# Gated linear attention and MLP: first loads in other pieces, and the fifth unit in another PSUM bank

## Chip, cores and metric

The kernel runs on one core of a Trainium2 chip. The metric is the device time of one execution in microseconds. It is written in Bass with every instruction's place on its engine given by a hand-written list; semaphores are derived from the dependencies. The engines are TensorE (PE), VectorE (DVE), ScalarE (ACT), GpSimd (POOL) and SyncE (SP, which only issues DMAs). Each runs its own list in order and waits for semaphores of the others.

## The reference

2048 tokens `x` of width 512. Branch `a` is linear attention with 32 heads of 16, whose features are the softmax of a projection and of its negative; branch `b` is a ReLU MLP with 1376 hidden columns. A sigmoid gate per token mixes them. (Types are bfloat16; heads and transposes are left out here.)

```python
def reference(x, wqkv, w_phi, wo, w1, w2, gate_w):
    g = sigmoid((x * gate_w).sum(-1, keepdims=True))
    q, k, v = split_heads(x @ wqkv)
    pq, pk = (einsum("bhsd,hdf->bhsf", t, w_phi) for t in (q, k))
    phi_q = concatenate([softmax(pq), softmax(-pq)], -1)
    phi_k = concatenate([softmax(pk), softmax(-pk)], -1)
    kv = einsum("bhsf,bhsd->bhfd", phi_k, v)
    z = einsum("bhsf->bhf", phi_k)
    o = einsum("bhqf,bhfd->bhqd", phi_q, kv) / (einsum("bhqf,bhf->bhq", phi_q, z)[..., None] + 1e-6)
    a = merge_heads(o) @ wo
    b = maximum(x @ w1, 0) @ w2
    return g * a + (1 - g) * b
```

## The kernel before

**Tiles.** Tokens are handled in 4 chunks of 512 and 16 tiles of 128. `XT` holds x transposed (512 columns as 4 slices of 128 partitions). Chunks 1 to 3 are transposed by DMA. Chunk 0 is loaded as it is, into a slot of the later feature buffer `FT` (seen as `XN`), and PE turns it in 128x128 blocks (`xt{m}{n}`: tile m, half n); ACT and DVE copy the blocks to `XT` (`xe{m}{n}`).

**Units.** A list of 48 units goes through PSUM. Unit `h{c}_{k}` (line 397) is the hidden block k of chunk c, 4 matmuls of 512 columns; `rl{c}_{k}` on ACT is its ReLU into `HT`. The eleventh block, k = 10, has 96 hidden rows and one more, the gate's logit, which DVE copies out (`gr{c}`, line 464); it goes through DRAM (`g1`, `g2`) to come back by token. Four units `f0_{j}` in chunk 2 fold `w_phi` into the query weights (line 374); the same for the keys (`f1_{j}`) is done near the start, outside the list of units. The units' order is chunk 0 with 10 blocks; chunk 1 with 10 and then both eleventh blocks, `h0_10` and `h1_10`; chunk 2 with 11 and the 4 folds; chunk 3 with 11. So `h3_10` is unit 47, counted from 0.

**Banks.** Of eight PSUM banks, the units use 3, 4, 5 (`HB`) and, for unit 3, bank 2; `freed[b]` remembers what has to be done before bank b is used anew:

```python
GB4 = (*HB, 2)
b = GB4[n] if n < 4 else HB[(n - 4) % len(HB)]
...
freed[b] = (f"rl{a}_{k}",)
if k == KT - 1:
    ...
    freed[b] += (f"gr{a}",)
```

Banks 0, 1, 6, 7 (`XB`, `FB`) serve the turning of chunk 0 and the key folds, later 0 and 1 the projections and 6 and 7 the key-value sums. After the units, the output tiles `b{m}` (second MLP matmul, 11 matmuls, line 628) and `a{m}` (attention output, line 634) take banks `AB = (3, 4, 5, 2)` in turn, and b0 to b2 wait for what `freed` names last for their bank:

```python
war = [f"oe{m - len(AB)}"] if m >= len(AB) else [f"ve{NT - 1}"] if ab == 2 else list(freed[ab])
```

**The opening.** The first chunk's hidden blocks 0 to 3 begin before it is all there: `hh00`, `hh01`, `hh1`, `hh2`, `hh3` (line 403) are the slices j of the contraction for tiles 0 and 1, each wanting its slice of W1's first 512 columns; `hr0`, `hr1` and the units `h0_0` to `h0_3` (line 409) are the rest. Six warming matmuls (`warm0`, line 258) run before data is there.

**The queues.** Loads are issued by SP and ACT. An issue takes its place in the engine's list. Behind the first ones SP issues `w1b` (W1's next 512 columns), `wphi`, `wkT` (key weights, transposed by DMA, wanted by the key folds), `w1c`, `wv` and the transposed chunks.

**The middle.** Work on keys (`pr_k`, `ev`, `mx`, `mn`, `t1`, `t2`, `ex`, `sm`, `rc`, `nm`) ends in `kv0` to `kv15` (PE, line 563). DVE then masks the sums (`kn0`, `kn1`, line 594; `kz0`, `kz1`, line 596). Queries go the same way, are transposed by DMA (`tq`), and `nd{m}_{h}` (PE, line 606) makes numerators and denominators, `rd` and `o` (DVE, lines 613 and 615) divide, `to` transposes, `a{m}` follows, `oe{m}` (ACT) scales and `st{m}` stores. In the lists this part reads as follows, with what comes before and after left out:

```python
"pe":  "... v15 kv14 h3_10 pr_q5 kv15 b0 nd0_0 nd0_1 b3 nd1_0 nd1_1 b2 pr_q6 a0 nd2_0 nd2_1 b1 nd3_1 ..."
"dve": "... sm_q1 kn1 kn0 kz0 kz1 rc_q1 mn_q4 gr3 rd0_1 rd0_0 o0_0 o0_1 sm_q2 rd1_0 ..."
```

## Time and profile before

| | |
|---|---|
| median of 3 runs | 151.53 us (151.14 to 152.31) |
| span of the profiled execution, first to last instruction | 150.2 us |
| PE busy | 145.2 us, 97% |
| DVE, POOL, ACT busy | 76%, 73%, 61% |
| granted TensorE clock | 0.9 or more in all 40 slices |
| loads: HBM read | 4.42 MB |

The time of the profiled execution itself is not listed beside its span; the median of the runs is 1.3 us above the span, for what lies around it. In a line of the timeline the columns are the start, the busy time (of a group, from its first start to its last end), engine, source line, operation, output and input, shape, count, and in brackets the idle time just before and what ended it. PEld is PE's loading of weights, which overlaps its matmuls; SPq and ACTq are DMA issues. The DMA view gives the time from issue to landing by size and queue.

### The profile page before, as it was taken

The numbers are of one execution on the slowest core, as the hardware profiler recorded it, in microseconds if no ns is written. First come the engines' busy times: TensorE is split into PE (matmuls) and PEld (weight loads), VectorE is DVE, ScalarE is ACT, GpSimd is POOL, SyncE is SP. The second block draws the span as 40 slices with busy tenths as digits, with TensorE's granted clock in tenths as the row PEclk, the third lists the DMA queues.
The fourth block names the chain that finished last, engine by engine and source line by source line (L and its number), as shares of the span: only waits on it lengthen the run. The fifth ranks groups of instructions, "written<-read, shape, count | busy, mean of one in ns | idle before, by whom it ended". The sixth has DMA issues, their size and how long they took to land.

```text
span 150.2 us, 2515 instructions
## 1 busy us (share of the span) xinstructions
PE 145.2 (97%) x944; PEld 74.2 (49%) x961; DVE 113.4 (76%) x168; ACT 92.2 (61%) x127; POOL 109.4 (73%) x71
## 2 busy tenths in 40 slices
PE   7899999999999999999999999999999999999992
PEld 3664444445554465445444545445444454454461
DVE  2433666999899949979999899999999969436301
ACT  3356769799969766698983937446546551310151
POOL 3000499999999999999999999998999791330000
PEclk9999999999999999999999999999999999999999
DMA  4999995000005602300000230476698774986251
GB/s 146 280 179 233 213 203 108 0 0 0 7 1 132 218 4 66 103 0 0 4 0 0 56 86 18 92 175 140 174 110 173 179 209 105 109 212 140 64 162 53
DMA packets 46307, 15.59 MB, mean 104 GB/s; under 512 B 39796, under 2 KB 46292, under 8 KB 46296
## 3 DMA queue, kind: packets, MB, share of 16 engines
q1 hardware_dynamic: 43560, 12.99, 42.0%
q10 hardware_dynamic: 2736, 2.45, 5.1%
q8 instruction: 7, 0.11, 0.4%
q14 instruction: 4, 0.03, 0.1%
HBM read 4.42 MB, written 2.11 MB: 43 GB/s over the span
## 4 chain that ended last, share of the span: by engine, by line
PE 93%; DMA 3%; issue 1%; ACT 1%; SPq 1%; DVE 0%
PE PS L628 24%; PE PS L397 23%; PE PS L502 18%; PE PS L482 9%; PE PS L634 9%; PE PS L563 3%; PE PS L606 3%; DMA W<-in_B_w_dram 3%; PE PS L649 2%; PE PS L374 1%; ACT HT L460 1%; PE PS L403 1%; PE PS L660 1%; SPq L272 1%; PE PS L409 0%
## 5 line engine op out<-in xcount | busy, mean ns | idle before, releaser
L542 POOL TENSOR_TENSOR TS<-PB,MX 128x1024 bf16<-128x1024 bf16 (+1 forms) x18 | 30.9, 1723 | 14.9 <-DVE MX L533 14.9
L397 PE MATMUL PS<-XT,W 128*128 128x512 bf16 (+1 forms) x156 | 38.3, 379 | 0.2
L628 PE MATMUL PS<-W,HT 128*128 128x512 bf16 (+1 forms) x160 | 37.5, 379 | 0.3
L549 DVE TENSOR_REDUCE ZB<-FT 128x128 f32<-128x2048 bf16 (+1 forms) x18 | 36.6, 2031 | 1.0 <-ACT FT L547 1.0
L547 ACT ACTIVATE FT<-TS 128x2048 bf16<-128x2048 bf16 (+1 forms) x18 | 30.9, 1718 | 7.7 <-POOL TS L542 7.5
L542 POOL TENSOR_TENSOR TS<-MN,PB 128x1024 bf16<-128x1024 bf16 (+1 forms) x18 | 30.9, 1724 | 0.8 <-DVE MN L535 0.8
L502 PE MATMUL PS<-WP,XT 128*128 128x512 bf16 x124 | 30.0, 379 | 0.2
L556 POOL TENSOR_TENSOR FT<-FT,SC 128x2048 bf16<-128x2048 bf16 (+1 forms) x9 | 29.5, 3290 | 0.0
L460 ACT ACTIVATE HT<-PS 128x512 bf16<-128x512 f32 (+1 forms) x44 | 24.7, 597 | 5.8 <-PE PS L397 4.9
L628 PEld LDWEIGHTS PS<-W,HT 128*128 128x128 bf16 (+1 forms) x165 | 15.5, 98 | 17.1
L533 DVE TENSOR_REDUCE MX<-PB 128x64 bf16<-128x1024 bf16 (+1 forms) x18 | 19.5, 1085 | 5.8 <-ACT PB L529 5.7
L397 PEld LDWEIGHTS PS<-XT,W 128*128 128x128 bf16 (+1 forms) x160 | 15.6, 101 | 16.5
L679 ACT ACTIVATE OSB<-PS,OMG 128x512 bf16<-128x512 f32 x15 | 10.2, 687 | 20.3 <-PE PS L634 20.3
L535 DVE TENSOR_REDUCE MN<-PB 128x64 bf16<-128x1024 bf16 (+1 forms) x18 | 19.3, 1084 | 2.3 <-ACT PB L529 2.3
L529 ACT ACTIVATE PB<-PS 128x1024 bf16<-128x1024 f32 (+1 forms) x18 | 16.7, 927 | 6.7 <-PE PS L502 3.8
L502 PEld LDWEIGHTS PS<-WP,XT 128*128 128x128 bf16 x128 | 12.1, 98 | 13.9 <-DVE WP L344 0.4
L579 POOL TENSOR_TENSOR FT<-FT,SR 128x1024 bf16<-128x1024 bf16 (+1 forms) x9 | 15.6, 1739 | 0.7
L482 PE MATMUL PS<-WV,XT 128*128 128x512 bf16 x62 | 16.0, 379 | 0.1
L634 PE MATMUL PS<-WO,OT 128*128 128x512 bf16 x58 | 14.2, 378 | 0.1
L615 DVE SCALAR_TENSOR_TENSOR OTM<-PS,EG,RD 128x256 bf16<-128x256 f32 x32 | 13.8, 463 | 0.2
L613 DVE RECIPROCAL RD<-PS 128x16 f32<-128x16 f32 x32 | 6.5, 235 | 9.0 <-PE PS L606 8.8
L491 ACT ACTIVATE VS<-PS 128x512 bf16<-128x512 f32 x16 | 9.6, 603 | 4.8 <-PE PS L482 4.7
(50 smaller groups left out, 97.8 us busy)
## 6 DMA issues: line engine op xcount, KB each, us to landing
out_dram<-OSB ACTq DMA_DIRECT2D x15, 128.0 KB, 2.1
W<-in_B_w_dram SPq DMA_DIRECT2D x1, 1280.0 KB, 6.7
W<-in_B_w_dram SPq DMA_DIRECT2D x1, 512.0 KB, 5.6
WV<-in_A_wqkv_dram SPq DMA_DIRECT2D x1, 512.0 KB, 4.7
WO<-in_A_wo_dram SPq DMA_DIRECT2D x1, 512.0 KB, 4.7
FT<-in_A_x_dram SPq DMA_DIRECT2D x3, 128.0 KB, 4.0
W<-in_B_w_dram SPq DMA_DIRECT2D x1, 352.0 KB, 3.9
W<-in_B_w_dram ACTq DMA_DIRECT2D x2, 128.0 KB, 3.7
```

Source lines behind the costliest of these rows:

```text
L397: last = q.matmul(PS[0:m, b, :], W1[:, j, k * P:k * P + m], XT[:, j, chunk(c)], start=(j == 0), stop=(j == ND - 1))
L460: add(f"rl{a}_{k}", "act", lambda q, a=a, k=k, b=b, rows=rows: q.activation(HT[0:rows, k, chunk(a)], PS[0:rows, b, :], ACT.Relu), (prev,), ...
L482: last = q.matmul(PS[:, 2, :], XT[:, j, m * P:(m + 1) * P], WV[:, j, :], start=(j == 0), stop=(j == ND - 1))
L502: last = q.matmul(PS[:, n, :], XT[:, j, m * P:(m + 1) * P], WP[:, s, j, :], start=(j == 0), stop=(j == ND - 1))
L533: add(f"mx_{J}", "dve", lambda q, sl=sl, w=w, i=pbg: q.tensor_reduce(MX[:, sl, 0:w * H], i, AX.X, ALU.max), (f"ev_{J}", old("t1")), dur=0. ...
L535: add(f"mn_{J}", "dve", lambda q, sl=sl, w=w, i=pbg: q.tensor_reduce(MN[:, sl, 0:w * H], i, AX.X, ALU.min), (f"ev_{J}", old("t2")), dur=0. ...
L542: add(f"{tn}_{J}", "pool", lambda q, o3=o3, a3=a3, b3=b3: q.tensor_tensor(o3, a3, b3, ALU.subtract), (f"{'mx' if sg == 0 else 'mn'}_{J}", ...
L547: add(f"ex_{J}", "act", lambda q, fs=fs, ts=ts, w=w: q.activation(FT[:, fs, 0:w * F], TS[:, ts, 0:w * F], ACT.Exp), (f"t1_{J}", f"t2_{J}", ...
L549: add(f"sm_{J}", "dve", lambda q, fs=fs, sl=sl, w=w: q.tensor_reduce(ZB[:, sl, 0:2 * w * H], FT[:, fs, 0:w * F].rearrange("p (g d) -> p g ...
L556: add(f"nm_{J}", "pool", lambda q, f3=f3, sl=sl, w=w: q.tensor_tensor(f3, f3, SC[:, sl, 0:2 * w * H].unsqueeze(2).to_broadcast([P, 2 * w * ...
L628: last = q.matmul(PS[:, ab, :], HT[0:r, k, m * P:(m + 1) * P], W2[0:r, k, :], start=(k == 0), stop=False)
L634: last = q.matmul(PS[:, ab, :], OT[:, m % NOT, t, :], WO[:, t, :], start=False, stop=(t == ND - 1))
```

## The change

Five edits go together.

- Chunk 0 is loaded in two pieces, both on SP, in each of which partition p takes rows 2p and 2p + 1 of 256 rows, so a packet is 2 KB and no longer 1 KB. Tile m of chunk 0 thus holds every second row, and the stores of tiles 0 to 3 go to the same rows (`stored`).
- W1's first 512 columns come in three pieces on ACT: slice 0, slice 1, and slices 2 and 3 in one. Before, x and these slices were spread over SP (x00, w1a0, w1a2, x02, x03) and ACT (x01, w1a1, w1a3).
- SP's later loads follow right behind the two pieces of x, so they go out earlier.
- On PE, `hh2` stands behind `xt31` and no longer ahead of `xt20`.
- Unit 4 (`h0_4`) takes bank 6 in place of bank 3, and the units behind it take `HB` counted from 5. `f1_2`, which uses bank 6 too, waits for `rl0_4`, and `rl0_4` moves ahead of `fe1_1` on ACT. The definition of the key folds moves behind that of the units.

```diff
 "sp":
-        "x00 w1a0 w1a2 x02 x03 w1b wphi wkT w1c wv x1 x2 wqT x3 gw ...
+        "x0a x0b w1b wphi wkT w1c wv x1 x2 wqT x3 gw ...
 "act":
-        "x01 w1a1 w1a3 xe00 xe10 xe20 xe30 rl0_0 rl0_1 rl0_3 rl0_2 fe1_1 fe1_3 rl0_5 rl0_4 ev_k0 ...
+        "w1a0 w1a1 w1a2 xe00 xe10 xe20 xe30 rl0_0 rl0_1 rl0_3 rl0_2 rl0_4 fe1_1 fe1_3 rl0_5 ev_k0 ...
 "pe":
-        "warm0 xt00 xt01 xt10 xt11 hh00 hh01 hh1 hh2 xt20 xt21 xt30 xt31 hh3 hr0 hr1 ...
+        "warm0 xt00 xt01 xt10 xt11 hh00 hh01 hh1 xt20 xt21 xt30 xt31 hh2 hh3 hr0 hr1 ...

+        def stored(m):
+            if m < 4:
+                return o2[m // 2 * 2 * P:(m // 2 + 1) * 2 * P, :].rearrange("(p n) d -> p n d", n=2)[:, m % 2, :]
+            return o2[m * P:(m + 1) * P, :]

-        load_x(0, "sp", 2.95)
-        load_x(1, "act", 3.1)
-        load_w(0, "sp", 3.2)
-        load_w(1, "act", 3.4)
-        load_w(2, "sp", 3.8)
-        load_w(3, "act", 3.95)
-        load_x(2, "sp", 4.0)
-        load_x(3, "sp", 3.9)
+        for n in range(2):
+            load(f"x0{'ab'[n]}", "sp", FT[:, NF - 2, n * 2 * D:(n + 1) * 2 * D],
+                 x2[n * 2 * P:(n + 1) * 2 * P, :].rearrange("(p m) d -> p (m d)", m=2), dur=0.45, lat=2.95)
+        for n, js in enumerate((slice(0, 1), slice(1, 2), slice(2, ND))):
+            load(f"w1a{n}", "act", W1[:, js, 0:512], w1r[:, js, 0:512], dur=0.45, lat=3.0)

+        freed[FB[2]] = ("xe30",)

-            b = GB4[n] if n < 4 else HB[(n - 4) % len(HB)]
+            b = GB4[n] if n < 4 else FB[2] if n == 4 else HB[(n - 5) % len(HB)]

-            war = [f"xe{2 + j // 2}{j % 2}"]
+            war = [f"xe{2 + j // 2}{j % 2}"] + (["rl0_4"] if j == 2 else [])

-                        out=o2[m * P:(m + 1) * P, :], in_=OSB[:, m % NOS, :]), (f"oe{m}",), dur=0.5, lat=1.5, dma=True)
+                        out=stored(m), in_=OSB[:, m % NOS, :]), (f"oe{m}",), dur=0.5, lat=1.5, dma=True)
```

The waits of `xt`, `hh` follow the new pieces' names (`x0a` for tiles 0 and 1, `x0b` for 2 and 3; `w1a2` for `hh2` and `hh3`). The lists are otherwise as they were, and so is `AB`.

## The prediction

> I expect the changed kernel to be slower, and not because of the loads. The loads shift little; the shift of one PSUM bank at the start runs through the whole list of units and ends at a new wait of TensorE (PE) in the middle.

> **What bounds the kernel now.** I read the first part of the page first, then the chain that ended last, then the timeline of the opening and of the stretch where the last ReLU unit hands its bank on. The page:

> ```profile
> span 150.2 us, 2515 instructions
> PE 145.2 (97%) x944; PEld 74.2 (49%) x961; DVE 113.4 (76%) x168; ACT 92.2 (61%) x127; POOL 109.4 (73%) x71
> PE 93%; DMA 3%; issue 1%; ACT 1%; SPq 1%; DVE 0%
> ```

> PE is busy for 97% of the span and 93% of the last chain is PE. Busy time by stretch puts 0.39 us of PE's idle time between 3.30 and 8.00 us, 0.05 in 8 to 13, and 0.37 in the 59.30 us from 88.00 to 147.30. PE executes its list in order, and it is the bound right to the end. So a delay of PE anywhere after 13 us has nothing behind it that would absorb it, and a gain can come from the opening alone. The opening:

> ```profile
> 3.34 0.77 PEld L350 LDWEIGHTS PS<-IDN,FT 128*128 128x128 bf16 x8 [0.76 <-DMA FT<-in_A_x_dram]
> 4.12 4.60 SPq L277 DMA_TRANSPOSE WT<-in_A_wqkv_dram  x1
> 5.87 0.60 PE L403 MATMUL PS<-XT,W 128*128 128x256 bf16 x4 [0.39 <-DMA W<-in_B_w_dram]
> 6.85 0.60 PE L403 MATMUL PS<-XT,W 128*128 128x256 bf16 x4
> 10.83 0.90 PEld L374 LDWEIGHTS PS<-WBD,WT 128*128 128x128 bf16 x16 [0.38 <-DMA WT<-in_A_wqkv_dram]
> ```

> The reader sees PE starting on x at 3.34 us, one wait for W1 (hh2 at 5.87), hh3 at 6.85, and the folds (L374) going as soon as wkT has landed, at 4.12 + 6.7 = 10.8 us. The middle:

> ```profile
> 87.45 0.42 PE L563 MATMUL PS<-VS,FT 128*128 128x65 bf16 x8
> 87.71 2.54 PE L628 MATMUL PS<-W,HT 128*128 128x512 bf16 x11
> 90.09 0.42 PE L606 MATMUL PS<-KVN,PHQ 128*128 128x68 bf16 x8
> ```

> kv15, then b0 (L628) directly behind it, then nd0. On DVE at the same time:

> ```profile
> 85.53 2.29 DVE L549 TENSOR_REDUCE ZB<-FT 128x128 f32<-128x2048 bf16 x1 [0.45 <-ACT FT L547]
> 87.91 0.76 DVE L594 TENSOR_TENSOR KVN<-PS,MK 128x256 bf16<-128x256 f32 x2
> 88.58 0.30 DVE L596 SCALAR_TENSOR_TENSOR KVN<-PS,MK 128x16 bf16<-128x16 f32 x2
> 88.74 0.54 DVE L573 RECIPROCAL SC<-ZB 128x64 f32<-128x64 f32 x1
> 89.20 1.16 DVE L535 TENSOR_REDUCE MN<-PB 128x64 bf16<-128x1024 bf16 x1
> 90.39 0.70 DVE L464 TENSOR_SCALAR GROW<-PS 1x512 f32<-1x512 f32 x1
> ```

> The last row is gr3, the gate row of the last chunk. It ends at 90.39 + 0.70 = 91.09 us, and everything above it from L594 on stands ahead of it in DVE's order and starts after kv15.

> **The banks.** Forty-eight units take banks in turn: 10 in chunk 0, 12 in chunk 1, 15 in chunk 2, 11 in chunk 3; h3_10 is unit 47. Before, its bank is HB[(47 - 4) % 3] = HB[1] = 4. With unit 4 moved to bank 6 the others take HB[(n - 5) % 3], so unit 47 gets HB[0] = 3. Among the units nothing changes, since each still waits for the one three ahead of it. But b0 to b2 take banks 3, 4, 5 by a fixed list that the diff leaves alone, and wait for what last freed them. Before, b0 waited for rl3_9 and b1 for rl3_10 and gr3; b1 stands far down PE's list, behind b0, nd0, b3, nd1, b2, pr_q6, a0 and nd2. After, b0 itself waits for gr3. PE's list keeps b0 right behind kv15, and gr3 stands on DVE behind kn and kz, which wait for kv15.

> The price: gr3 ends at 91.09. From a DVE release to the first matmul the trace shows 0.16 us (the fold's copy ends at 11.27 + 1.29 = 12.56, the projection's first matmul is at 12.72). So b0 starts at 91.25 instead of 87.71: **3.54 us**. Queued behind b0 on PE are nd0, b3, nd1, b2, pr_q6 and a0. DVE waits for nd0 (rd0), ACT for pr_q6 and a0, so they wait too, each by at most the same 3.54. I let nothing be regained: L628 has no idle time before it, and the waits of PE's weight loads for transposed tiles add to 0.7 us over the whole run, with matmuls running over them. Bounds: 3.2 (rows alone, from PE's end at 87.87 to gr3's end at 91.09) and 3.7.

> **The loads.** SP issues seven loads ahead of wkT before, four after. Rows of issues are 0.41 to 0.51 us, some 0.47 with their spacing, so wkT and w1b go out 3 x 0.47 = 1.4 us earlier. ACT issues three both times. What PE needs in order is x0a, w1a0, w1a1, x0b, w1a2.
> x0a is two pieces in one: the old first two landed at 0.74 + 2.6 = 3.3 and 0.75 + 2.7 = 3.5. In the same time now come x0a and w1a0, half as many bytes again, so x0a lands at 3.3 to 3.7, and xt00 starts up to 0.4 late. That alone doesn't reach the end, as hh2 still waits.
> hh2 now stands behind xt20 to xt31 and needs 256 KB, w1a2. hh2 and hh3 take 4 matmuls each at 0.109 (an earlier half of 8 took 0.87), 0.44 per step. Old hh3 started at 6.85; the same point is kept if hh2 starts at 6.85 - 0.44 = 6.41, that is, if w1a2 lands by 6.28 (landing to matmul 0.14: 5.73 to 5.87). Low bound: w1a2 as the old third piece, 1.67 + 4.06 = 5.73, gain 0.55. High bound: all 1.05 MB of x and W1 landed by 2.61 + 4.0 = 6.6; if w1b, now 1.4 us earlier on the other queue, is served alternately with w1a2, 0.26 MB more go first, 1.0 us at the 271 GB/s of the 3.3 to 8 us stretch: 7.6, loss 1.3. That 2 KB packets go faster no row shows (there are hardly any of them), so I let them gain nothing. I take 6.5, **a loss of 0.2**, nearer the middle than either end.
> [...]
> A gain is capped by wkT: the folds wait for it now with no slack, and it lands no earlier than the bytes ahead of it on its queue allow. They are as many as before, less the W1 pieces that went to ACT and were served beside it anyway. Between 0 and 1.4 us earlier, enough for the 0.55.

> **Edits that I price at nothing.** h0_4 in bank 6 waits for xe30 (done by 7.4, needed after 9). f1_2 now waits for rl0_4: ACT's four ReLUs before it end at 8.16 + 2.18 = 10.34, rl0_4 takes 0.60, so 10.94; f1_2 is the third fold, at 11.3. Cover 0.36; without it, up to 0.3. The strided stores of tiles 0 to 3 move as many bytes in 1 KB rows; they land in 2.1 us, and st0 issued at 107.25 is needed at 115.23 (oe5). Bounds 0 and, at four times the landing, about 0.4.

> **The clock.** At the start the six 512-column matmuls took 2.72 us, 0.45 each, against 1.73 / 8 = 0.22 later. So PE starts at half speed and was granted all of it by about 4.3 us, after 3.5 us of work. Whether an idle stretch of 3.4 us costs the clock no row shows; the longest wait that PE has after 4.3 is 0.39 (at 5.87). Bounds: 0, and half of 3.5 us, 1.75. I take 0, as PE was working shortly before and after.
> [...]

> **Sum.** +3.54 +0.2 = +3.7 on the span of 150.2, so 153.9. The list of times does not say which of them is the profiled execution's own; the median, 151.53, lies 1.3 above the span for what is around it, and carries over: **155.3 us**.

> **Rivals.**
> - The same wait, and the clock lost (in the stall, or at the start through a longer gap before xt00): 155.3 + 1.75 = 157.0. For it: the size of the stall. Against: the work on both sides.
> - The same wait, with w1a2 late behind w1b: 155.3 + 1.1 = 156.4. For it: the loads of the opening landed one behind the other up to 6.6, so bytes count. Against: ACT's W1 pieces landed close to SP's, issued at the same time.
> - The same wait, with the opening improved: 155.3 - 0.2 - 0.55 = 154.5.
> - The other side: b0 does not wait, so only the opening counts, and the 0.39 us hole at hh2 with the small ones near it is closed: 151.53 - 0.55 = 151.0, no slower. It decides if gr3 is done before 87.7, that is, if DVE ran it ahead of kn. h3_10 ends by 86 and its ReLU by 87.5, so the data would allow it; DVE's written order does not. This is also the case in which the change does what it says. Faster by over 1% would need 1.5 us, more than all of PE's idle time from 3.3 to 13 us.

> **Chances.** The forecast 0.64, late w1a2 0.10, lost clock 0.10, better opening 0.09, no wait 0.07. A measurement of this kernel tells about 1% (1.5 us) from no change. Faster 0.02 and same 0.05 come from the last case; slower 0.93 is the rest. The range reaches from the better opening, less 0.5 for the spread of the runs before, to the lost clock: 154.0 to 157.0.

> **What would show it.** Right: an idle of 3.2 to 3.7 us on PE ahead of the first L628 of the changed profile, released by the gate row on DVE; b0's start some 3.5 us further behind kv15; DVE idle about 2.5 us ahead of the first reciprocal L613. hh2's step shows w1a2, and the matmul spacing behind b0 shows the clock. Wrong: b0 running directly behind kv15, or a total under 153.

## The result, and the profile after

The changed kernel takes 157.67 us (median, 156.83 to 158.08) against 151.74 for the kernel before on the same chip: a ratio of 1.037, with a 95% interval of 1.035 to 1.040. It is slower by 5.9 us; 155.3 was forecast, and 157.67 lies above the range. A ratio leaves out executions over 1.5% above the kernel's fastest, which matters below for three kernels with a larger spread than that (AB alone, the split W1 and the 1 KB packets, the last two with six warming matmuls).

The page of the profiled execution (span 156.1), with the same three lines as before:

```profile
span 156.1 us, 2511 instructions
PE 147.5 (94%) x944; PEld 75.5 (48%) x961; DVE 113.5 (73%) x168; ACT 92.3 (59%) x127; POOL 109.5 (70%) x71
PE 91%; DMA 4%; DVE 2%; issue 1%; ACTq 1%; DVEq 0%
```

PE has more idle time, but also 2.3 us more busy time with the same 944 matmuls. So they ran slower somewhere, and the row of the granted clock shows where most of it is, at slices 24 and 25 of 40:

```profile
PEclk9999999999999999999999977999999999999999
```

That is 1.5 of the 2.3 us. The rest lies in the opening, where the row can't show it: its records begin with the full clock, at 6.72 us here and at 4.34 in the profile before, and the first twelve matmuls of L393 took 1.89 us and not 1.26. It cost nothing there, since PE waits for W1 behind them.

All that PE waited for is in four lines (engine and line, what it waited for, us in total, times, longest):

```profile
PE PS L625 <- DVE GROW L454: 3.4, 1, 3.4
PE PS L263 <- PEq L729: 0.8, 1, 0.8
PE PS L345 <- DMA FT<-in_A_x_dram: 0.6, 1, 0.6
PE PS L393 <- DMA W<-in_B_w_dram: 0.4, 1, 0.4
```

L625 is the line of b0 now, L454 the gate row gr3, L393 hh. The stretch in the timeline, first PE, then the end of the chain on DVE:

```profile
88.62 0.42 PE L560 MATMUL PS<-VS,FT 128*128 128x65 bf16 x8
92.41 4.03 PE L625 MATMUL PS<-W,HT 128*128 128x512 bf16 x11 [3.36 <-DVE GROW L454]
96.27 0.42 PE L603 MATMUL PS<-KVN,PHQ 128*128 128x68 bf16 x8
```

```profile
90.38 1.16 DVE L532 TENSOR_REDUCE MN<-PB 128x64 bf16<-128x1024 bf16 x1
91.56 0.70 DVE L454 TENSOR_SCALAR GROW<-PS 1x512 f32<-1x512 f32 x1
96.73 0.37 DVE L610 RECIPROCAL RD<-PS 128x16 f32<-128x16 f32 x2 [4.47 <-PE PS L603]
```

The loss can be read off by comparing starts with the profile before:

| step | before | after | lost |
|---|---|---|---|
| start of kv15 (all that is ahead of it) | 87.45 | 88.62 | 1.17 |
| kv15 to b0 | 0.26 | 3.79 | 3.53 |
| b0 to nd0 | 2.38 | 3.86 | 1.48 |
| nd0 to the last copy on DVE | 57.26 | 57.27 | 0.01 |
| behind that copy's start (the last stores) | 2.85 | 2.56 | -0.29 |

Their sum is 5.90, the difference of the spans. The same eleven matmuls of b0 took 1.48 us longer, and the clock by stretch says why (PE busy, PEld, DVE, ACT, POOL, PEclk, DMA share, GB/s):

```profile
89.00:92.40 3.40, 0.04 (x2) 0.02 (x1) 3.15 (x7) 1.19 (x1) 3.32 (x4) 0.95 0.04 8
92.40:95.40 3.00, 2.99 (x8) 1.05 (x9) 0.00 (x0) 1.63 (x2) 3.00 (x3) 0.50 0.00 1
```

So there are three parts: the opening, the wait, and the clock behind the wait. The opening in the timeline:

```profile
4.06 1.03 PE L345 MATMUL PS<-IDN,FT 128*128 128x128 bf16 x8 [0.57 <-DMA FT<-in_A_x_dram]
7.64 1.05 PE L393 MATMUL PS<-XT,W 128*128 128x256 bf16 x8 [0.37 <-DMA W<-in_B_w_dram]
12.02 1.06 PE L369 MATMUL PS<-WBD,WT 128*128 128x128 bf16 x16
```

xt00 at 4.06 and not 3.34, hh2 at 7.64, as soon as w1a2 had landed (7.60), and not 5.87 (with more work ahead of it now; the forecast had put its break-even at 6.41), and the folds at 12.02 without any wait for wkT, which landed at 9.3.

### The profile page after: what moved, and what is told of

Same layout as the page of the kernel before. It is cut to its first block, busy times and chain, and to the rows that moved or that the text cites. A ratio compares the mean times of both kernels' runs of the same rounds, so it can differ in the third digit from the quotient of the medians.

```text
span 156.1 us, 2511 instructions
## 1 busy us (share of the span) xinstructions
PE 147.5 (94%) x944; PEld 75.5 (48%) x961; DVE 113.5 (73%) x168; ACT 92.3 (59%) x127; POOL 109.5 (70%) x71
## 4 chain that ended last, share of the span: by engine, by line
PE 91%; DMA 4%; DVE 2%; issue 1%; ACTq 1%; DVEq 0%
PE PS L625 24%; PE PS L387 22%; PE PS L499 18%; PE PS L479 9%; PE PS L631 8%; DMA W<-in_B_w_dram 4%; PE PS L560 3%; PE PS L603 3%; PE PS L646 2%; PE PS L369 1%; PE PS L399 1%; DVE MN L532 1%; PE PS L393 1%; PE PS L657 1%; ACTq L277 1%
## 5 line engine op out<-in xcount | busy, mean ns | idle before, releaser
L625 PE MATMUL PS<-W,HT 128*128 128x512 bf16 (+1 forms) x160 | 39.0, 390 | 3.6 <-DVE GROW L454 3.4
L625 PEld LDWEIGHTS PS<-W,HT 128*128 128x128 bf16 (+1 forms) x165 | 15.8, 100 | 21.7 <-issue 5.4
```

The source lines that it names most:

```text
L625: last = q.matmul(PS[:, ab, :], HT[0:r, k, m * P:(m + 1) * P], W2[0:r, k, :], start=(k == 0), stop=False)
```

## Experiments on the three parts

**Each half of the change alone.** First the changed kernel with the banks as they were:

```diff
-            b = GB4[n] if n < 4 else FB[2] if n == 4 else HB[(n - 5) % len(HB)]
+            b = GB4[n] if n < 4 else HB[(n - 4) % len(HB)]
```

(`freed[FB[2]]` and f1_2's wait for rl0_4 go with it.)

> The changed kernel with unit 4 back in bank 3, so h3_10 is back in bank 4 and b0 waits for rl3_9 alone. My theory: the changed kernel's loss is a sum of three, the opening +1.2 us, the wait of b0 for the gate row +3.5, and the half clock behind that wait +1.5 where it falls. Then this kernel keeps only the opening: 151.7 + 1.2 = 152.9 us, no idle time of PE ahead of b0, full clock behind it. Rival (the wait comes from the late opening, with the gate row's place on DVE shifted against PE, and not from the bank): about 156 to 158, the idle time ahead of b0 stays at 3.4.

Measured: 152.98 us, ratio 1.006 (1.004 to 1.008), span 150.7. PE doesn't wait ahead of b0, and the clock is full behind it (2.38 us from b0 to nd0, and a granted clock of 0.999 or 1.000 in all five executions). Then the kernel before, with the bank change alone:

```diff
-            b = GB4[n] if n < 4 else HB[(n - 4) % len(HB)]
+            b = GB4[n] if n < 4 else FB[2] if n == 4 else HB[(n - 5) % len(HB)]
-        "... rl0_3 rl0_2 fe1_1 fe1_3 rl0_5 rl0_4 ev_k0
+        "... rl0_3 rl0_2 rl0_4 fe1_1 fe1_3 rl0_5 ev_k0
```

(and f1_2's wait.)

> The kernel before with the bank change alone (unit 4 in bank 6, the others counted from 5, f1_2 waiting for rl0_4, rl0_4 earlier on ACT); loads and PE's order as before. My theory: the opening as before, b0 3.5 us later, and 1.5 us more where the clock falls: 151.7 + 3.5 to 5.0 = 155.2 to 156.7. Rival (the bank is harmless and the loads do it all): 151.7.

Measured: 157.15 us, ratio 1.033 (1.030 to 1.037). Its timeline has the loads of before and the whole of the wait:

```profile
87.47 0.42 PE L564 MATMUL PS<-VS,FT 128*128 128x65 bf16 x8
91.26 3.89 PE L629 MATMUL PS<-W,HT 128*128 128x512 bf16 x11 [3.37 <-DVE GROW L459]
94.99 0.42 PE L607 MATMUL PS<-KVN,PHQ 128*128 128x68 bf16 x8
```

kv15 starts where it did before (87.45), b0 3.53 us late, and b0 takes 3.73 in place of 2.38, with a granted clock of 0.989 in each of its four executions. So one bank moved by one unit at the start costs 5.1 us, some 80 microseconds later, and the rest of the change costs 0.95. The two halves add up to 6.05, against 5.9 for both. The rival, a wait that comes of the late opening, has fallen.

**The same change without the wait.**

```diff
-    NDB, AB = (6, 7), (3, 4, 5, 2)
+    NDB, AB = (6, 7), (4, 5, 3, 2)
```

> The changed kernel with the output tiles' banks in another order, AB = (4, 5, 3, 2): b0 and b1 then take the banks freed long ago, and b2, which stands behind b3 and nd1, takes bank 3 with the gate row's wait. If the wait of b0 for the gate row is what costs, it vanishes with all else of the change kept: 152.9, PE without idle time ahead of b0. Rival (moving unit 4 or rl0_4 costs by itself, or the wait only moves on to b2): 154 to 156.

Measured: 152.59 us, ratio 1.004 (1.002 to 1.006). One of the ten executions took 155.44 us with a granted clock of 0.989; it was not profiled, so where its clock fell without this wait stays open. In the profiled one (span 150.5) PE doesn't wait ahead of b0. Moving unit 4 and rl0_4 cost nothing that shows; what cost is that the list which hands banks to the output tiles was written for the old rotation. b2 now has the wait for gr3, and meets it when gr3 is long done:

```profile
88.04 0.42 PE L560 MATMUL PS<-VS,FT 128*128 128x65 bf16 x8
88.30 2.54 PE L625 MATMUL PS<-W,HT 128*128 128x512 bf16 x11
90.67 0.42 PE L603 MATMUL PS<-KVN,PHQ 128*128 128x68 bf16 x8
```

**The clock by itself.** PE is given work while b0 waits, on constants and into a bank that is free:

```diff
-        "... pr_q5 kv15 b0 nd0_0
+        "... pr_q5 kv15 fill b0 nd0_0
+        g.add("fill", "pe", lambda q: pe_warm(q, 15 * (512,)), (f"ve{NT - 1}", "rl0_3"), dur=3.24)
```

> The changed kernel with 15 matmuls of 512 columns on constants put between kv15 and b0, into bank 2, which is free then; they take 15 x 0.216 = 3.24 us, so PE works through the time in which b0 waits for the gate row, and b0 starts when it did. Their result is overwritten. My theory of the clock: it fell to half because PE was idle, so it stays full here, b0 takes 2.5 us and not 4.0, and the span is 156.1 - 1.5 = 154.6 (156.2 us) in every execution. Rival (the half clock comes from something else, or its loss is hidden): span 155.4 to 156.1 with a granted clock of 0.989 in some executions.

Measured: 156.32 us, span 154.1 to 154.5, granted clock 0.998 or 1.000 in all four. The ratio is 1.028 (1.026 to 1.030) where the changed kernel has 1.037: idle time replaced by useless work makes it 1.35 us faster by the medians. Not all of that is the fallen clock: the three executions of the changed kernel without a fall (156.83 to 157.65) are slower than the filled kernel too. The size of the clock's part is read from the profiles, b0 to nd0:

```profile
88.36 3.44 PE L263 MATMUL PS<-const-bfloat16-1.0 128*128 128x512 bf16 x15
91.89 2.54 PE L625 MATMUL PS<-W,HT 128*128 128x512 bf16 x11
94.26 0.42 PE L603 MATMUL PS<-KVN,PHQ 128*128 128x68 bf16 x8
```

b0 starts 3.79 us behind kv15 as in the changed kernel, but takes 2.37 to nd0. With half the filling:

> The changed kernel with 7 matmuls of 512 columns between kv15 and b0 in place of 15: PE works for 1.5 us of the wait and is idle for 1.8 to 1.9. The profiles showed the clock falling at the end of a 3.41 us period in which PE had worked 12%, 20% and 36% of it. Here no period can be below 45%. Theory 1 (a period must be mostly idle): no fall, all clocks 1.000, as with 15, 156.3. Theory 2 (a period needs three quarters of work, as it seems to at the start): the clock falls in about every second execution, 156.3 in some and 157.8 in others.

Measured: 156.41 us (156.0 to 157.29), PE idle for 1.84 ahead of b0, granted clock 0.998 or more in all four executions; no fall, as the first theory has it. The changed kernel once more:

> The changed kernel once more, for one look. Some of its executions show a granted clock of 0.989 (spans 155.7 to 156.1), others 1.000 (154.9 to 155.6). By my theory one with 0.989 has an idle time ahead of b0 that covers nearly a whole period of the clock's watch, and one with 1.000 has it split between two; the second kind should be 1.5 us shorter with the same opening, about 154.5. Rival: the clock's fall is hidden in the idle time, and both kinds have the same length but for the opening.

Measured: span 156.9 and a granted clock of 0.978, neither of the two kinds. The half clock held for two periods:

```profile
88.00:90.50 2.50, 0.48 (x10) 0.29 (x7) 2.41 (x7) 0.05 (x1) 2.50 (x2) 1.00 0.27 60
92.00:94.00 2.00, 2.00 (x6) 0.65 (x5) 0.00 (x0) 1.46 (x2) 2.00 (x2) 0.50 0.00 1
94.00:97.00 3.00, 3.00 (x16) 1.32 (x15) 0.00 (x0) 0.33 (x1) 2.63 (x2) 0.50 0.00 0
```

In the clock records of the first profile the full clock runs from 6.72 to 92.05 us, 25 times 3.413 us, the half clock from there to 95.46, once 3.413, and the full one again to 156.90, 18 times; in the profile before the full clock runs from 4.34 to 151.11, 43 times (151.11 and 156.90 lie just behind the ends of the spans). Here the half clock runs from 90.65 to 97.48, twice. Call 3.41 us a period. Counted back from these changes, the first whole period of the span begins at 0.92 us in the profile before, at 3.30 in the first one and at 1.90 here, so elsewhere in each. Here the clock fell at the end of a period in which PE had worked until 88.48, 36% of it, and did not come back at the end of the next one, with 65% of work (from b0's start at 91.85), but after a full one. In the first profile it fell after a period with 12% of work, with the bank alone after one with 20%, and it came back after periods with 89% (b0 from 92.41 to 95.46) and 81%. In the half filled kernel the period with the idle time had 46% of work, and the clock stayed. The expectation that a wait of 3.4 us costs either 1.5 or nothing was too simple: the executions have one period at half speed (mean clock 0.989), two (0.978), or none (1.000). These profiles fit that the place of the wait in the periods decides which; that is the author's reading, and no run here moves the wait alone. None of the changed kernel's executions with a mean of 1.000 (spans 154.9 to 155.6) was profiled. The half filled kernel, with the same loads and the same start of b0, spans 154.2 to 155.5 without a fall, and in its profile (154.8) w1a2 landed as late as 7.80. So the spread of the opening is enough for nearly all of their length, but that it was the cause is not shown; the late full clock of the next section is another candidate, since the mean counts only from the first record on (the first profile's 0.989 is its 3.41 us at half clock behind the wait and nothing of the opening).

## Experiments on the opening

All of these keep AB = (4, 5, 3, 2), so the opening alone differs from the kernel before. First, w1b goes out on ACT behind w1a2, on the same queue:

```diff
 "sp":
-        "x0a x0b w1b wphi wkT ...
+        "x0a x0b wphi wkT ...
 "act":
-        "w1a0 w1a1 w1a2 xe00 ...
+        "w1a0 w1a1 w1a2 w1b xe00 ...
```

> The kernel with AB = (4, 5, 3, 2) and w1b moved from SP to ACT, behind w1a2 on the same queue, so that it can't be served ahead of it; behind x0b SP has wphi and wkT, whose packets are 256 B. My theory (w1b takes half of the turns from w1a2): w1a2 lands some 0.6 us earlier than with AB alone, hh2 at about 6.4 and not 7.06; w1b lands about 8 and is wanted only after 9. 152.6 - 0.6 = 152.0. Rival (the queue of ACT is slow by itself): hh2 stays at 7.0 and the time at 152.6.

Measured: 151.93 us, ratio 1.001 (1.000 to 1.003). The DMA views (KB, us from issue to landing) have w1a2 at 5.3 us with AB alone and at 4.6 here:

```profile
W<-in_B_w_dram ACTq DMA_DIRECT2D x1, 256.0 KB, 5.3
```

```profile
W<-in_B_w_dram ACTq DMA_DIRECT2D x1, 256.0 KB, 4.6
```

```profile
6.33 1.05 PE L393 MATMUL PS<-XT,W 128*128 128x256 bf16 x8
```

The first line is AB alone, the second w1b on ACT, and the third is from the timeline of the latter: hh2 starts at 6.33 without a wait, against 7.06. So w1b, brought forward by 1.4 us on the other queue, delayed w1a2 by 0.7 us in these two profiles; the ratios, 1.004 and 1.001, have intervals that overlap. The third experiment shows that it was not the only cause. (The packets of wphi are 32 B, not 256 as the expectation says; nothing rests on it.) Second, W1's last slices apart, one of them on SP ahead of w1b:

```diff
-        "x0a x0b w1b wphi ...
+        "x0a x0b w1a3 w1b wphi ...
-        for n, js in enumerate((slice(0, 1), slice(1, 2), slice(2, ND))):
-            load(f"w1a{n}", "act", W1[:, js, 0:512], w1r[:, js, 0:512], dur=0.45, lat=3.0)
+        for n in range(ND):
+            load(f"w1a{n}", "act" if n < 3 else "sp", W1[:, n, 0:512], w1r[:, n, 0:512], dur=0.45, lat=3.0)
```

> The kernel with AB = (4, 5, 3, 2) and the last W1 piece split: slice 2 stays on ACT, slice 3 goes to SP right behind x0b and ahead of w1b; hh2 and hh3 wait for their own slices. My theory of the opening: w1a2's 256 KB share the time with w1b's 512 KB on the other queue, turn by turn, so they land when nearly all of the 1.5 MB has moved (about 7.0). Here only the 1 MB that PE needs first is ahead of w1b, so the last of it should land at 6.0 to 6.3 and hh2 start by 6.2: the opening 0.8 to 1.0 us shorter than with AB alone, 152.6 - 0.9 = 151.7 us, level with the kernel before. Rival (w1a2 is late because of the 2 KB packets of x or the start of the queues, not of w1b): no earlier than 6.8, 152.4 to 152.8.

Measured: 151.81 us against 151.89, ratio 0.999 (0.997 to 1.001), no measurable difference from the kernel before. Two of the twelve executions took 153.86 and 154.02 us; they come up again below. In the profile the last of the slices landed at 5.86, and hh2 follows xt31 at once:

```profile
3.95 0.62 PE L345 MATMUL PS<-IDN,FT 128*128 128x128 bf16 x8 [0.46 <-DMA FT<-in_A_x_dram]
6.10 1.04 PE L393 MATMUL PS<-XT,W 128*128 128x256 bf16 x8
```

Third, the packets: x in the same pieces, but in 1 KB packets (the stores of tiles 0 to 3 then go to rows in order again).

```diff
-            load(f"x0{'ab'[n]}", "sp", FT[:, NF - 2, n * 2 * D:(n + 1) * 2 * D],
-                 x2[n * 2 * P:(n + 1) * 2 * P, :].rearrange("(p m) d -> p (m d)", m=2), dur=0.45, lat=2.95)
+            load(f"x0{'ab'[n]}", "sp", XN[:, n * 2:n * 2 + 2, :],
+                 x2[n * 2 * P:(n + 1) * 2 * P, :].rearrange("(m p) d -> p m d", p=P), dur=0.45, lat=2.95)
```

> The kernel with AB = (4, 5, 3, 2) and x's first 512 tokens in the same two pieces on SP, but in 1 KB packets (tile m takes rows in order, the stores too). My theory: the queues take turns packet by packet, so SP's 2 KB packets gave x two thirds of the bytes against W1 on ACT. With 1 KB each, x and W1 move evenly, so x0a lands later (4.0 or more), W1's pieces earlier against x, and w1a2 competes with w1b less: hh2 at 6.3 to 6.6, 152.6 - 0.5 = 152.1. Rival (2 KB packets simply move faster, and that outweighs the turns): everything later by some 0.2, 152.8.

Measured: median 153.54 us, in two groups, 151.7 to 151.9 (two) and 153.4 to 154.2 (seven). In the profile, one of the long group, w1a2 landed at 6.2, early enough for the forecast start of hh2, and x0a at 4.24. So with equal packets w1a2 landed at 6.2 and not at 7.0, as with AB alone, though w1b is where it was: the 2 KB packets and the early w1b delayed it together. Of the turns that the theory speaks of the trace shows packet counts: in the first profile SP's queue moved 84 packets of 2 KB (x) and ACT's 79 of 1 KB (W1) from 2.6 to 3.3 us, 0.17 and 0.08 MB, and from 5.0 to 6.0 us 201 and 175, all of 1 KB. In what order a DMA engine takes them is not shown. The first group is near the forecast time, the second a surprise. The profile:

```profile
4.28 1.04 PE L345 MATMUL PS<-IDN,FT 128*128 128x128 bf16 x8 [0.79 <-DMA FT<-in_A_x_dram]
7.69 1.92 PE L393 MATMUL PS<-XT,W 128*128 128x256 bf16 x8
```

hh2 and hh3 take 1.92 us, against 1.05 in the other kernels, and no load holds them up: the full clock came only at 10.06 us. PE had been idle from 3.5 to 4.3, and the two periods before, which ended at 3.23 and 6.65, had 72% and 77% of work. In the split W1 profile the full clock came after a period with 78%. So the opening can lose time to the clock too, here 0.87 us at hh2 and hh3. The test is longer warming (`WARM = (8 * (512,),)`), meant to end as x0a lands:

> x in 1 KB packets as before in this study, with eight warming matmuls, which end at 0.77 + 8 x 0.427 = 4.19, just ahead of the first transposes at 4.28. With six, the profiled execution got the full clock only at 10.06 us, as PE was idle from 3.5 to 4.3, and seven of nine took 153.4 to 154.2, two 151.7 to 151.9. My theory: it was the clock alone, so nearly all executions take 151.7 to 152.2 here. Rival (1 KB packets are slower to land): the median stays at 153.5.

Measured: 152.11 us (151.81 to 152.6, ten executions), ratio 1.003 (1.000 to 1.005). The long group is gone, though x0a landed no earlier; in the profile it landed at 4.59, xt00 started at 4.63, PE was idle for only 0.29 us ahead of it, and the full clock came at 5.40. With the split W1 and seven warming matmuls:

> AB = (4, 5, 3, 2), W1 in four pieces with slice 3 on SP ahead of w1b, and seven warming matmuls in place of six, so PE works until 0.77 + 7 x 0.427 = 3.76 us, just ahead of x0a (3.9), and the first period of the clock's watch has nearly no idle time in it wherever it begins. With six, most executions took 151.3 to 152.2 us and two 153.9 to 154.0. My theory: those two got the full clock one period of 3.4 us later, since PE had been idle from 3.3 to 3.9. Then none is over 152.5 here, and the median is 151.6. Rival (the long ones come from the loads): some 1 in 6 stay near 154.

Measured: 151.89 us (151.52 to 152.54, twelve executions), ratio 1.002 (1.000 to 1.004). No execution near 154 any more, as expected, but the median did not fall to 151.6, and two in twelve is too few for their absence to prove much. In the profile w1a2 landed at 6.77, against 5.86 with six warming matmuls, and hh2 started at 6.82 after a wait of 0.58; why these loads came later is not known. So the opening, mended, brings the change level with the kernel before; no version here beats it.

## Why the prediction was wrong, point by point

- **The wait: right.** The rotation of banks, the list AB that didn't follow, gr3 as the releaser, 3.54 us: measured 3.53, and the same with the bank alone. Nothing of it was regained on PE, as the sum assumed: nd0 to the last copy is the same to 0.01 us. DVE waited 4.47 us for nd0, not 2.5; 1.48 of the difference is b0's slower run.
- **The clock: the step that failed.** "I take 0, as PE was working shortly before and after" let the work around the gap decide. The clock fell all the same, with gaps of 3.36 and 3.37 us and with 12%, 20% and 36% of work in the 3.41 us before the fall. The term measured 1.48 and 1.35 us in the profiled executions of the change and of the bank alone, and nothing where the wait was filled (b0 to nd0 2.37). On the span the sum gave 153.9 and the profile 156.1: the clock's term was short by 1.48, the opening's by 0.97, and the last stores gave back 0.29. The clock stood in the text as a rival at 0.10; four of seven executions of the changed kernel and all four of the bank alone show it.
- **The opening: the mechanism right, the value wrong.** The text had the case of w1b served alternately with w1a2, gave 7.6 us for it as the late end of w1a2's landing, and then took 6.5 for being near the middle. The alternation was an estimate there; the first profile shows 201 packets on SP's queue and 175 on ACT's from 5.0 to 6.0 us. Measured: 7.60 in the first profile, 7.0 to 7.2 in four others with these loads and 7.80 in a fifth (half filled), so between the forecast and the late end in most, and at the late end or past it in two. The term was 0.2, and it was 0.59 and 0.74 in the two profiles without the wait, 1.17 in the first; by the medians, 0.56 and 0.95. Moving w1b to ACT bears the mechanism out: w1a2 then landed at 6.3. The larger share of x's 2 KB packets, 0.17 MB against 0.08 from 2.6 to 3.3 us, was not in the sum. (The 1.1 of the rival is the 1.3 of that late end less the 0.2 taken.)
- **x0a** landed at 4.0, later than the 3.3 to 3.7 given, and wkT 1.5 us earlier than before, a little over the 1.4 that was given as the most.
- **The range.** Late w1a2 and the lost clock were treated as alternatives, at 156.4 and 157.0. Nothing excluded both; together they give 158.1, and this is where the executions with the fallen clock lie (157.7 to 158.8). The range had to reach there. Of the executions without a fall (156.83, 157.27, 157.65), two lie above 157.0 too, so the fallen clock is not all that the range lacked.
- **The edits priced at nothing** cost nothing that can be told from the rest: with AB changed alone, the kernel keeps all of them and its median is 0.56 us above the kernel before, where the opening of its profile lost 0.59.

## What to carry to other kernels

When a buffer rotation is shifted, follow it to its last user: whatever takes the buffers over by a fixed list inherits other dependencies, and PE, which ran its list in order, lost the whole 3.53 us of the slowest. In these profiles w1b, 1.4 us earlier on one queue, went with w1a2 0.7 us later on the other, so a load that an early matmul needs is worth trying ahead of it (hh2 at 6.10) or on the same queue (6.33, against 7.06). A wait of PE of 3.36 us cost 1.48 us more behind it, at half clock, while b0 took its 2.38 us behind one of 1.84, so a long wait is better priced with what may follow it. The rivals of a forecast should be added up where nothing makes them exclusive.
